# A linear-attention and MLP block on one core: own tile for the last group's sums, a low part behind the first addition, output weights behind the reciprocals, another bank

## The chip, the core and the metric

The kernel runs on one core of a Trainium2 chip. A core has TensorE for matrix products (PE in the profile; its weight loads are PEld), VectorE (DVE), ScalarE (ACT), GpSimd (POOL) and SyncE (SP), which here issues nearly all DMAs. Each engine works off its own queue in order and waits for the others by semaphores. PE writes into PSUM, eight banks of 128 x 512 float32 numbers; DVE and ACT read the banks and free them. The metric is the device time of one execution in microseconds (us); a lower time is better.

## What is computed

One block with two branches on the same normalized input; S = 2048 tokens, D = 640 channels, 32 heads of 20, a hidden layer of 1728, all in float32:

```python
def reference(A_x, A_wqkv, A_w_phi, A_wo, B_x, B_w1, B_b1, B_w2, B_b2):
    x = A_x
    xn = _layernorm(x, axis=-1)
    return x + _A_ref(xn, A_wqkv, A_w_phi, A_wo) + _B_ref(xn, B_w1, B_b1, B_w2, B_b2)

def _A_ref(x, wqkv, w_phi, wo):
    q, k, v = ...                       # x @ wqkv, split into 32 heads
    pq, pk = q @ w_phi, k @ w_phi       # by head
    phi_q = concat(softmax(pq), softmax(-pq))
    phi_k = concat(softmax(pk), softmax(-pk))
    num = phi_q @ (phi_k^T v)
    den = phi_q . sum_s(phi_k) + 1e-6
    return (num / den) @ wo

def _B_ref(x, w1, b1, w2, b2):
    y = _layernorm(x, axis=-1)
    return gelu(y @ w1 + b1) @ w2 + b2
```

## The kernel before

**Split products.** Every float32 operand is split exactly into two parts of the type float32r: a high part, which ACT rounds, and a low part, the rest, which DVE or POOL subtracts (`split`, line 51). A product of two operands takes three matmuls (`mm3`): high by high on line 64, high by low on line 65, low by high on line 66. Nearly all of PE's work has these three lines, in the MLP, the projections and the output product alike.

**The MLP.** Tokens are cut into four blocks `b` of 512, the hidden layer into seven groups `g` of two tiles `j` of 128 (the last group has one and a half). A pass (`passes`, line 255) has two halves: the first layer for the two tiles (five triples of matmuls each into one bank, then gelu on ACT, its high part on ACT and its low part on DVE), and behind a `yield` the second layer: five output tiles `m`, each of six matmuls into a bank, which DVE adds to the accumulator `acc` (line 295 in the first group, 297 later). The halves of neighbouring passes interlock: the first half of a pass is written ahead of the second half of the pass before it. So the low parts of a pass are needed only one pass later. Three banks (0, 1, 2, called `ph`) serve the first layer, two (3, 4, `px`) whatever runs beside it, three (5, 6, 7, `po`) the second layer; output tile `m` + 3 can start only when the addition of tile `m` is done.

**Beside the MLP.** `beside` is a generator, one step of which is taken after each triple; with it, other work is laced into the queues of PE, ACT, DVE and POOL at fixed places, whose order on these engines is the order of writing. What runs beside is, in turn: the transposes of the second token block (`next_y`, line 408, to which `make_y01` belongs, line 173 for the transposes); the preparation of folded weights (L467) and of the later token blocks (`prep`, L563 to L572); then the end of the key-value sums (`finish_kv`, products on lines 866 and 876); and the attention itself (`attend`). The order on SP is a scheduler's.

**Attention.** For each block, `groups` runs through group 10 (the last two heads, and the sums by which the quotients are formed) and then groups 0 to 9: `first` splits the features (L921 on ACT, L922 on POOL), `second` multiplies them with the key-value matrix (L928, L929), copies half of the bank to the tile `ts` on ACT (L938) and adds the other half to it on DVE (L939). For group 10 the result itself stands in `ts`, and two DMAs store it from there (L941, L942). `quotients` then collects the sums through DRAM, takes reciprocals (`dt`, L957), loads them in five transfers into the tile `rx` (L962, L965, L967), spreads them over partitions (L973 on DVE) and multiplies (L975 on POOL).

**Output product.** The weight `wo`, split earlier, is loaded back by `load_wo` (L1004, L1006) into the slots `w3`, `w1`, `r1`, `r2` when the pass (6, 2) has begun; `late` holds a raw copy of `wo` in two pieces (L1040) for sums of weights, with which the output product of blocks 2 and 3 saves matmuls. The output product follows the last pass, in two loops over output tiles.

Of the kernel before, what the change touches and what calls it, by code (L numbers as in the profile page):

```python
# [8 lines left out]
F32 = mybir.dt.float32  # L9
# [31 lines left out]
def f(ap):  # L41
    return ap.bitcast(F32)
# [3 lines left out]
def tile_kernel(ctx: ExitStack, tc: tile.TileContext, x, xT, wkT, wqT, wv, wphi, wo, w1, b1, w2, b2,  # L46
# [152 lines left out]
    class Mlp:  # L199
        def __init__(self, slots, hid):  # L200
            self.hid, self.turn, self.slots, self.beside, self.raw = hid, 0, slots, iter(()), {}
            self.ph, self.px, self.po = Banks(0, 1, 2), Banks(3, 4), Banks(5, 6, 7)

# [47 lines left out]
        def gelu(self, g, j, pz, gt, hh, hl):  # L251
            self.last = nc.scalar.activation(gt, pz, AF.Gelu_apprx_tanh, bias=b1t[:, 2 * g + j:2 * g + j + 1]).ins  # L252
            split(hh, hl, gt)

        def passes(self, g, b, ws, hid=None):
# [27 lines left out]
            for m in range(KC):  # L283
                pw = self.po()
                ms = slice(m * P, (m + 1) * P)
                for j, (hh, hl) in enumerate(hid):
                    w2h, w2l = ws[j][2:]
                    if hl is not None:
                        mm3(pw, w2h[:, ms], w2l[:, ms], hh, hl, j == 0, j == 1)
                        next(self.beside, None)  # L290
                    else:
                        nc.tensor.matmul(pw, w2h[:, ms], hh, start=False, stop=False)
                        nc.tensor.matmul(pw, w2l[:, ms], hh, start=False, stop=True)
                if g == 0:
                    nc.vector.scalar_tensor_tensor(acc[b][:, m, :], pw, b2t[:, m:m + 1], acc[b][:, m, :], op0=ALU.add, op1=ALU.add)
                else:
                    nc.vector.tensor_tensor(acc[b][:, m, :], pw, acc[b][:, m, :], op=ALU.add)  # L297

# [101 lines left out]
    for i in range(4):  # L400
        scale(4 + i, x1[i])
        zs[i]()
    for st in (s23, s47):
        step(st, 1)
# [3 lines left out]
    def next_y():  # L408
        ptile = Banks(3, 4, 0, 1)
        for _ in range(6):  # L410
            yield
        for half in range(2):
            for i, _ in enumerate(make_y01(1, half, x1[2 * half:2 * half + 2], ptile)):
                for _ in range(4 if (half, i) == (0, 1) else 2):
                    yield

    mlp.beside = next_y()
# [425 lines left out]
    def finish_kv(pxt):  # L843
# [30 lines left out]
        tp = pxt()  # L874
# [5 lines left out]
    class Attention:  # L880

        def __init__(self, b, bank):
            self.b, self.n, self.bank = b, 0, bank
            self.ob = op.tile([P, KC, 512], F32, name=f"ob{b}") if b < 2 else acc01.tile([P, KC, 512], F32, name=f"acc{b - 2}")
            self.ts = ep.tile([P, 512], F32, name="ts")
# [39 lines left out]
        def second(self, g, w, ph, pl):  # L925
# [9 lines left out]
            else:  # L935
                a, z = slice(0, 42), slice(64, 106)
                t = o = self.ts[a, :]
# [6 lines left out]
        def quotients(self):  # L944
# [54 lines left out]

    def load_wo():  # L1000

        for p, wd in enumerate(wo_dram):
            w = wp.tile([P, 4, D], F32R, name=f"w{(3, 1)[p]}")
            nc.sync.dma_start(f(w), wd[:, 0:4, :])  # L1004
            last = rp.tile([P, D], F32R, name=f"r{1 + p}")
            nc.sync.dma_start(f(last), wd[:, 4, :])  # L1006
            wol.append([w[:, kc, :] for kc in range(4)] + [last])
# [16 lines left out]
    wol, phs = [], []  # L1024
    ep = op = rx = None

    def attend():
# [73 lines left out]
    for g in range(7):  # L1101
        for b in range(2, 4):
# [17 lines left out]
            if (g, b) == (6, 2):  # L1120
                load_wo()
# [199 lines left out]
```

## Time and profile before

| | us |
|---|---|
| median of three runs | 725.42 |
| lowest and highest run | 723.91, 726.64 |
| the profiled execution | 726.09 |
| its span in the trace | 724.3 |
| PE idle for DVE, POOL (sum of the waits) | 8.9 |
| first matmul after the span's start | 1.3 |

Each row of a timeline has the start and the length in us, the engine, the line, the operation, what it writes and reads, and in brackets how long the engine sat idle before it and for whom. Matmuls overlap: each is shown until its result stands, but the next one starts earlier. In the view of waits a row says which line waited for which, for how long in all, how often, and the longest one. The TensorE clock was granted in full (1.00) throughout.

### The profile page before, as it was taken

Reading aid. Unit: us, or ns where it says so; the run is one execution under the profiler, and the core shown is the slowest. Engines: PE = TensorE matmul, PEld = TensorE weight load, DVE = VectorE, ACT = ScalarE, POOL = GpSimd, SP = SyncE. Lnnn points to the kernel's source line nnn. Section 1 sums busy time; section 2 is a strip of 40 time slices with the busy share of each in tenths; the row PEclk is TensorE's granted clock in tenths of the full one; section 3 lists DMA queues with packets and bytes.
Section 4 is the critical chain, followed back from the end, with each engine's and each line's share of the span. In section 5 each row is a group of like instructions: output and inputs, shape, how many; then the busy total and the mean of one; then the engine's idle time right before and its main releaser. Section 6 shows DMA issues by size and latency. Waiting matters only on the chain.

```text
span 724.3 us, 9717 instructions
## 1 busy us (share of the span) xinstructions
PE 712.1 (98%) x3402; PEld 598.0 (83%) x3402; DVE 488.0 (67%) x824; ACT 333.5 (46%) x569; POOL 388.7 (54%) x342
## 2 busy tenths in 40 slices
PE   9999999999999999999999999999999999999998
PEld 7788888778888888888888888777878778878887
DVE  7846655765554798798788798535574656869753
ACT  6624445433313563464454458346554556551310
POOL 2211222555202896896888878455586677554400
PEclk9999999999999999999999999999999999999999
DMA  9803675455151223723600705863435443163222
GB/s 326 273 19 108 191 198 183 172 179 179 64 209 82 93 71 151 178 91 148 144 1 11 171 1 196 223 159 100 124 109 164 139 145 106 43 233 117 78 82 88
DMA packets 67146, 96.86 MB, mean 134 GB/s; under 512 B 14657, under 2 KB 37841, under 8 KB 65473
## 3 DMA queue, kind: packets, MB, share of 16 engines
q1 hardware_dynamic: 66808, 96.23, 42.7%
q8 instruction: 27, 0.44, 0.3%
q14 instruction: 23, 0.18, 0.1%
q10 hardware_dynamic: 288, 0.01, 0.0%
HBM read 65.87 MB, written 30.35 MB: 133 GB/s over the span
## 4 chain that ended last, share of the span: by engine, by line
PE 77%; DMA 7%; POOL 4%; DVE 4%; issue 3%; ACT 3%; SPq 2%; POOLq 0%; DVEq 0%; ACTq 0%
PE bank L64 23%; PE bank L65 23%; PE bank L66 23%; DMA rx<-d 2%; PE bank L704 2%; DMA r<-in_w 2%; PE bank L467 2%; POOL w L58 1%; PE bank L929 1%; PE bank L928 1%; DMA xb<-in_x 1%; POOL ob L975 1%; DMA e<-e 1%; DVE st L130 1%; DMA o<-ts 1%
## 5 line engine op out<-in xcount | busy, mean ns | idle before, releaser
L58 POOL TENSOR_TENSOR w<-r,w 128x640 fp32r<-128x640 f32 x52 | 84.6, 1645 | 120.2 <-ACT w L55 89.8
L64 PE MATMUL bank<-y,w 128*128 128x512 f32 (+1 forms) x310 | 120.5, 389 | 0.0
L66 PE MATMUL bank<-y,w 128*128 128x512 f32 (+1 forms) x310 | 120.2, 388 | 0.0
L65 PE MATMUL bank<-y,w 128*128 128x512 f32 (+1 forms) x310 | 120.1, 388 | 0.0
L64 PE MATMUL bank<-m,w 128*128 128x512 f32 x266 | 105.6, 397 | 3.8 <-DVE acc L297 3.7
L66 PE MATMUL bank<-m,w 128*128 128x512 f32 x266 | 104.1, 391 | 0.0
L65 PE MATMUL bank<-m,w 128*128 128x512 f32 x262 | 102.4, 391 | 0.0
L58 DVE TENSOR_TENSOR m<-m,m 128x512 fp32r<-128x512 f32 (+1 forms) x54 | 45.0, 833 | 72.3 <-ACT m L55 72.2
L297 DVE TENSOR_TENSOR acc<-bank,acc 128x512 f32<-128x512 f32 x120 | 80.5, 682 | 16.4 <-PE bank L66 11.6
L64 PE MATMUL bank<-wkh,y 128*128 128x512 f32 (+2 forms) x240 | 87.6, 365 | 0.0
L65 PE MATMUL bank<-wkl,y 128*128 128x512 f32 (+2 forms) x240 | 87.1, 363 | 0.0
L66 PE MATMUL bank<-wkh,y 128*128 128x512 f32 (+2 forms) x240 | 86.9, 362 | 0.0
L65 PEld LDWEIGHTS bank<-y,w 128*128 128x128 f32 x310 | 58.3, 188 | 12.1
L66 PEld LDWEIGHTS bank<-y,w 128*128 128x128 f32 x310 | 58.2, 188 | 12.1
L64 PEld LDWEIGHTS bank<-y,w 128*128 128x128 f32 x310 | 58.2, 188 | 12.0
L669 POOL TENSOR_TENSOR m<-m,mx 128x640 f32<-128x640 f32 (+2 forms) x48 | 44.5, 940 | 42.7 <-DVE mx L657 42.7
L650 ACT ACTIVATE m<-bank 128x512 f32<-128x512 f32 (+1 forms) x64 | 26.5, 440 | 85.5 <-PE bank L66 59.6
L64 PEld LDWEIGHTS bank<-m,w 128*128 128x128 f32 x266 | 50.0, 188 | 17.1 <-DVE acc L297 6.9
L252 ACT ACTIVATE m<-bank,b1t 128x512 f32<-128x512 f32 (+1 forms) x54 | 36.3, 672 | 53.3 <-PE bank L66 50.7
L922 POOL TENSOR_TENSOR e<-e,m 120x512 fp32r<-120x512 f32 (+1 forms) x28 | 38.1, 1361 | 39.6 <-ACT m L921 39.0
L66 PEld LDWEIGHTS bank<-m,w 128*128 128x128 f32 x266 | 49.9, 188 | 10.7
L676 DVE TENSOR_REDUCE sm<-m 128x64 f32<-128x1280 f32 x32 | 47.3, 1479 | 15.9 <-ACT m L674 15.7
(213 smaller groups left out, 1468.2 us busy)
## 6 DMA issues: line engine op xcount, KB each, us to landing
r<-in_w SPq DMA_DIRECT2D x52, 320.0 KB
e<-e SPq DMA_DIRECT2D x40, 240.0 KB
e<-acc SPq DMA_DIRECT2D x52, 160.0 KB
acc<-in_xT SPq DMA_DIRECT2D x4, 1280.0 KB
xb<-in_x SPq DMA_DIRECT2D x8, 320.0 KB
t<-in_x SPq DMA_DIRECT2D x8, 320.0 KB
raw<-in_xT SPq DMA_DIRECT2D x10, 256.0 KB
yh<-t SPq DMA_DIRECT2D x10, 256.0 KB
```

Source lines behind the costliest of these rows:

```text
L58: eng.tensor_tensor(lo, src, f(hi), op=ALU.subtract)
L64: nc.tensor.matmul(ps, lh, rh, start=first, stop=False, **kw)
L65: nc.tensor.matmul(ps, lh, rl, start=False, stop=False, **kw)
L66: nc.tensor.matmul(ps, ll, rh, start=False, stop=last, **kw)
L252: self.last = nc.scalar.activation(gt, pz, AF.Gelu_apprx_tanh, bias=b1t[:, 2 * g + j:2 * g + j + 1]).ins
L297: nc.vector.tensor_tensor(acc[b][:, m, :], pw, acc[b][:, m, :], op=ALU.add)
L467: nc.tensor.matmul(ps[:, c + i * kd:c + (i + 1) * kd], raw[n, g][:kk, (kc + i) * P:(kc + i + 1) * P], wpt[:kk, g, :kd // DF, 1:], start=Tr ...
L650: return nc.scalar.activation(p3[:, :, c], ps.rearrange("p (h f) -> p h f", h=H), AF.Copy).ins
L669: subs[n, t] = nc.gpsimd.tensor_tensor(ep[:, s], a, b, op=ALU.subtract)
L676: nc.vector.tensor_reduce(sm, e.rearrange("p s (h f) -> p (s h) f", f=DH), axis=AX, op=ALU.add)
L704: nc.tensor.matmul(kvp[g // 2][:VM, (g % 2) * 240:(g % 2) * 240 + 240].rearrange("p (s f) -> p s f", s=4), v[:, g * VS:g * VS + VM], ft[:, ...
L922: nc.gpsimd.tensor_tensor(pl, e, f(ph), op=ALU.subtract)
```

## The change

Five edits.

1. Group 10's sums get a tile of their own, `rest`, in place of `ts`.
2. With the flag `hold`, the gelu of the second tile of a pass makes its high part at once, but its low part is kept back until the first addition of the second layer that is written next. The flag is set for the passes from (1, 0) on, left out for (2, 0), and in the second part of the kernel, which handles blocks 2 and 3, set from the attention on, at (1, 2): 20 low parts move.
3. At the start, the transposes `next_y` begin three steps later, and the last of four scalings of x goes from DVE to ACT, behind the gelus.
4. The third product of `finish_kv` (L876) takes its bank from `ph` (it becomes bank 0) where it took one from `px` (bank 3, which the first product had).
5. Of `load_wo` the two large loads move into `quotients` of the last block, behind the last load of reciprocals; the two small ones stay where they were (`load_last`). The two raw pieces of `wo` are issued later, at steps 24 and 28 of block 2's groups in place of 8 and 16.

```diff
         def gelu(self, g, j, pz, gt, hh, hl):
             self.last = nc.scalar.activation(gt, pz, AF.Gelu_apprx_tanh, bias=b1t[:, 2 * g + j:2 * g + j + 1]).ins
-            split(hh, hl, gt)
+            if self.hold and j == 1:
+                nc.scalar.activation(hh, gt, AF.Copy)
+                self.held.append(lambda: nc.vector.tensor_tensor(hl, gt, f(hh), op=ALU.subtract))
+            else:
+                split(hh, hl, gt)
...
                     nc.vector.tensor_tensor(acc[b][:, m, :], pw, acc[b][:, m, :], op=ALU.add)
+                while self.held:
+                    self.held.pop()()
...
     for i in range(4):
-        scale(4 + i, x1[i])
+        if i < 3:
+            scale(4 + i, x1[i])
         zs[i]()
+    scale(7, x1[3], True)
...
         ptile = Banks(3, 4, 0, 1)
-        for _ in range(6):
-            yield
-        for half in range(2):
-            for i, _ in enumerate(make_y01(1, half, x1[2 * half:2 * half + 2], ptile)):
-                for _ in range(4 if (half, i) == (0, 1) else 2):
+        for _ in range(9):
+            yield
+        for half, waits in enumerate(((3, 1, 1), (2, 2, 2))):
+            for n, _ in zip(waits, make_y01(1, half, x1[2 * half:2 * half + 2], ptile)):
+                for _ in range(n):
                     yield
 
-    mlp.beside = next_y()
+    mlp.beside, mlp.hold = next_y(), True
...
             this = mlp.passes(g, b, ws)
+            mlp.hold = (g, b) != (2, 0)
             next(this)
...
-        tp = pxt()
+        tp = mlp.ph()
...
-            self.ts = ep.tile([P, 512], F32, name="ts")
+            self.ts, self.rest = ep.tile([P, 512], F32, name="ts"), ep.tile([42, 512], F32, name="rest")
...
-                t = o = self.ts[a, :]
+                t = o = self.rest
...
-                nc.sync.dma_start(rx[o + 2::64], rden[30:32].unsqueeze(1).to_broadcast([2, KC, 512]))
+                last = nc.sync.dma_start(rx[o + 2::64], rden[30:32].unsqueeze(1).to_broadcast([2, KC, 512])).ins
                 yield
+            if self.b == NB - 1:
+                with tc.issue_after(last):
+                    load_wo()
...
-                    if b == 2 and i in (8, 16):
-                        j = i // 16
+                    if b == 2 and i in (24, 28):
+                        j = i // 28
...
-                mlp.beside = attend()
+                mlp.beside, mlp.hold = attend(), True
...
             if (g, b) == (6, 2):
-                load_wo()
+                load_last()
```

On PE, in the program's first part (`xb` are the token tiles, `y` the normalized input, `w_171` the second hidden tile's weights, `m` the hidden layer), there stands before, at the first transposes:

```order
L64 MATMUL bank_425<-y_141,w_171 128x512
L65 MATMUL bank_425<-y_142,w_171 128x512
L66 MATMUL bank_425<-y_141,w_171 128x512
L173 MATMUL bank_432<-idt,xb 128x128 x4
L64 MATMUL bank_425<-y_141,w_171 128x512
```

and now, three triples further on:

```order
L64 MATMUL bank_425<-y_141,w_171 128x512
L65 MATMUL bank_425<-y_142,w_171 128x512
L66 MATMUL bank_425<-y_141,w_171 128x512
L173 MATMUL bank_441<-idt,xb 128x128 x4
L64 MATMUL bank_450<-m_146,w_168 128x512
```

The first transposes have moved from inside the second tile's first layer to its end, right ahead of the second layer.

On DVE, at the end of the preparation (`raw` are columns of x, `m_1528` is the low part of the second gelu, `acc` the accumulator), before:

```order
L58 TENSOR_TENSOR m_1501<-m_1500,m_1501 128x512
L563 TENSOR_TENSOR raw<-raw,m_1247 128x512
L58 TENSOR_TENSOR m_1528<-m_1500,m_1528 128x512
L570 TENSOR_TENSOR raw<-raw,t 128x512
L297 TENSOR_TENSOR acc_99<-bank_1550,acc_99 128x512
L297 TENSOR_TENSOR acc_99<-bank_1564,acc_99 128x512
```

and now (line numbers of the changed kernel: 572 and 579 are the former 563 and 570, 302 is the former 297, 256 is the low part kept back):

```order
L58 TENSOR_TENSOR m_1501<-m_1500,m_1501 128x512
L572 TENSOR_TENSOR raw<-raw,m_1247 128x512
L579 TENSOR_TENSOR raw<-raw,t 128x512
L302 TENSOR_TENSOR acc_99<-bank_1549,acc_99 128x512
L256 TENSOR_TENSOR m_1528<-m_1500,m_1528 128x512
L302 TENSOR_TENSOR acc_99<-bank_1564,acc_99 128x512
```

The low part has moved behind the first addition; the other rows keep their order.

On SP, ahead of the output product (`dt` and `rx` are the reciprocals, `woh` and `wol` the split output weights), before:

```order
L958 DMA d_95<-dt 128x128
L962 DMA rx<-d_95 4x2560
L1004 DMA w_5849<-woh 128x2560
L1004 DMA w_5853<-wol 128x2560
L965 DMA rx<-d_95 2x2560
L967 DMA rx<-d_95 2x5x512
L965 DMA rx<-d_95 2x2560
L967 DMA rx<-d_95 2x5x512
```

and now:

```order
L968 DMA d_95<-dt 128x128
L972 DMA rx<-d_95 4x2560
L975 DMA rx<-d_95 2x2560
L977 DMA rx<-d_95 2x5x512
L975 DMA rx<-d_95 2x2560
L977 DMA rx<-d_95 2x5x512
L1024 DMA w_5891<-woh 128x2560
L1024 DMA w_5893<-wol 128x2560
```

The two loads of the weights have moved behind all five transfers of the reciprocals. At block 1's reciprocals the two pieces of `wo` (L1040 before), of which one stood between the transfers, both stand behind them now.

More of the change, by code (lines that the diff above doesn't have):

```diff
@@ L202, in __init__ @@
             self.ph, self.px, self.po = Banks(0, 1, 2), Banks(3, 4), Banks(5, 6, 7)
+            self.hold, self.held = False, []
         def fetch(self, c, pool=None):
@@ L998, in split, with load_last @@
                 nc.sync.dma_start(acc[b], a_dram[b])
+    def load_last():
+        for p, wd in enumerate(wo_dram):
+            last = rp.tile([P, D], F32R, name=f"r{1 + p}")
+            nc.sync.dma_start(f(last), wd[:, 4, :])
+            lasts.append(last)
     def load_wo():
@@ L1004, in load_wo @@
             nc.sync.dma_start(f(w), wd[:, 0:4, :])
-            last = rp.tile([P, D], F32R, name=f"r{1 + p}")
-            nc.sync.dma_start(f(last), wd[:, 4, :])
-            wol.append([w[:, kc, :] for kc in range(4)] + [last])
+            wol.append([w[:, kc, :] for kc in range(4)] + [lasts[p]])
     def first_split():
@@ L1022, in both @@
             yield
-    wol, phs = [], []
+    wol, lasts, phs = [], [], []
     ep = op = rx = None
```

## The prediction

> **What bounds the kernel now.** I read the page's first part, then the waits of TensorE (PE), then the timeline of PE around each wait.
>
> ```profile
> PE 712.1 (98%) x3402; PEld 598.0 (83%) x3402; DVE 488.0 (67%) x824; ACT 333.5 (46%) x569; POOL 388.7 (54%) x342
> PE bank L64 <- DVE acc L297: 3.7, 5, 1.4
> PE bank L173 <- DVE xb L164: 1.7, 2, 1.4
> PE bank L876 <- DVE km L858: 1.4, 1, 1.4
> PE bank L929 <- POOL e L922: 0.8, 1, 0.8
> ```
>
> PE works 98% of the span and no other engine comes near it. The matmuls are not changed, so only PE's holes can be won. The view of waits gives four kinds: the second-layer matmuls (L64) wait for a PSUM bank that an addition (L297) has not yet emptied, transposes (L173) wait for a scaled x, L876 waits for its bank, and one attention matmul (L929) waits for its low part. Together 7.6 us, but a hole costs more than its idle time, as one of them shows.
>
> ```profile
> 488.35 0.40 PE L66 MATMUL bank<-m,w 128*128 128x512 f32 x1
> 490.20 0.50 PE L64 MATMUL bank<-m,w 128*128 128x512 f32 x1 [1.45 <-DVE acc L297]
> 490.53 0.40 PE L65 MATMUL bank<-m,w 128*128 128x512 f32 x1
> 490.76 0.39 PE L66 MATMUL bank<-m,w 128*128 128x512 f32 x1
> ```
>
> In full flow a 512-column matmul starts 0.23 us after the one before (490.53 to 490.76), though each is shown 0.40 long. Before the hole the step is 490.20 - 488.35 = 1.85, so 1.62 is lost, and the next step (0.33) loses 0.10 more: 1.72 for 1.45 of idle. So I add 0.27 to each idle time, or 0.16 where the next step is a normal one.
>
> ```profile
> 26.38 0.55 PE L173 MATMUL bank<-idt,xb 128*128 128x128 f32 x3 [1.42 <-DVE xb L164]
> 131.39 0.50 PE L64 MATMUL bank<-m,w 128*128 128x512 f32 x1 [0.33 <-DVE acc L297]
> 159.17 0.50 PE L64 MATMUL bank<-m,w 128*128 128x512 f32 x1 [0.28 <-DVE acc L297]
> 460.83 0.56 PE L876 MATMUL bank<-sel,kxs 107*80 107x30 f32 x6 [1.37 <-DVE km L858]
> 539.90 0.40 PE L66 MATMUL bank<-m,w 128*128 128x512 f32 x1
> 540.36 0.50 PE L64 MATMUL bank<-m,w 128*128 128x512 f32 x1
> 573.17 0.51 PE L64 MATMUL bank<-m,w 128*128 128x512 f32 x1 [0.78 <-DVE acc L297]
> 586.68 0.50 PE L929 MATMUL bank<-e,kvs 120*128 120x512 f32 x1 [0.78 <-POOL e L922]
> 650.80 0.50 PE L64 MATMUL bank<-m,w 128*128 128x512 f32 x1 [0.88 <-DVE acc L297]
> ```
>
> The prices: 1.58 at 26 us, 0.60 at 131, 0.55 at 159, 1.53 at 461, 1.72 at 490, 0.33 at 540 (a step of 0.46 for 0.23, and 0.10), 1.05 at 573, 1.05 at 587, 1.15 at 651. **Ceiling: 9.6 us.** Each hole is now asked whether the change closes it, and what comes next there.
>
> **The transposes (26 us), -1.4.** The first ones move from behind the 7th first-layer triple to behind the 10th, three triples of 3 x 0.23 later.
>
> ```profile
> 24.69 0.27 PE L173 MATMUL bank<-idt,xb 128*128 128x128 f32 x1
> 25.79 0.54 DVE L164 TENSOR_SCALAR xb<-xb,ry 128x640 f32<-128x640 f32 x1
> 27.05 0.42 DVE L58 TENSOR_TENSOR m<-m,m 128x256 fp32r<-128x256 f32 x1
> 28.36 0.69 ACT L252 ACTIVATE m<-bank,b1t 128x512 f32<-128x512 f32 x1 [1.49 <-DVE ra L153]
> ```
>
> They would start at 24.69 + 2.04 = 26.73; the second x they need is scaled at 26.33. The hole goes. But PE now reaches the second layer at about 27.1 (26.73 and some 0.4 for four transposes, an estimate from the 0.55 that three take with their modelled tail), and its second matmul, 0.23 later, needs the low part that DVE ends at 27.47: I charge 0.2 for that; bounds 0 and 0.5. The last scaling, moved from DVE to ACT, falls into the 1.49 that ACT waits for DVE ahead of the next gelu, and shortens that wait by the 0.54 that DVE no longer spends on it. I count nothing for it; without that cover ACT would be late by a scaling, somewhat over the 0.69 of a gelu.
>
> **Low part behind the addition (131, 159), -1.15.** In the 20 places where the order of DVE changes, the low part of the second gelu stands behind the first addition.
>
> ```profile
> 157.22 0.69 DVE L58 TENSOR_TENSOR m<-m,m 128x512 fp32r<-128x512 f32 x1 [1.94 <-ACT m L55]
> 158.44 1.28 DVE L297 TENSOR_TENSOR acc<-bank,acc 128x512 f32<-128x512 f32 x2
> ```
>
> DVE sat idle for 1.94 with the addition queued behind a low part that waited for ACT. Without it the addition can run up to 1.94 sooner, and sooner by the 0.69 of the low part in any case; 0.55 was missing. At 131 the order changes in the same way, and 0.60 was missing, less than a low part. Both holes go; bounds 0 and 1.15. The low part itself is read only in the next block's second layer, many us later.
>
> **Bank of L876 (461), -1.4.** Three products share two banks, so the third waited for DVE to read the first. Taken from the three banks of the first layer, it starts at once. Next in line is the first attention group:
>
> ```profile
> 473.73 1.29 POOL L922 TENSOR_TENSOR e<-e,m 80x512 fp32r<-80x512 f32 x1 [12.70 <-ACT m L921]
> 476.56 0.40 PE L929 MATMUL bank<-e,kvs 80*128 80x512 f32 x1
> ```
>
> POOL ends at 475.02, on a chain from loads that do not move with PE. PE asked at 476.56 and will ask at 476.56 - 1.53 = 475.03: just met, so I charge 0.1; bounds 0 and 1.5.
>
> **Own tile for the sums (490), -1.7.** The sums of group 10 stood in the tile `ts`, which the next group overwrites.
>
> ```profile
> 479.53 4.57 DMA o<-ts
> 484.21 0.60 ACT L938 ACTIVATE ts<-bank 64x512 f32<-64x512 f32 x1 [6.10 <-PE bank L66]
> ```
>
> The chain of waits shows ACT held until the store had read `ts` (the bracket names the wrong one of several waits); a gelu, a low part and the addition came late behind it. With `rest` ACT can go on up to 6.1 us sooner, as soon as PE has filled the bank; 1.72 was missing. Bounds 0 and 1.72.
>
> **The output weights' pieces (573), -1.05, and what hangs on it (587), -0.3.**
>
> ```profile
> 563.22 0.39 SPq L1040 DMA_DIRECT2D woc<-in_wo  x1
> 564.86 6.64 DMA rx<-d
> 571.63 0.01 DVE L973 LOAD_MASK_SELECT rx<-rx  x1 [1.82 <-DMA rx<-d]
> 572.47 2.67 POOL L975 TENSOR_TENSOR ob<-ob,rx 128x512 f32<-128x512 f32 x2 [1.36 <-DVE rx L973]
> 584.90 1.73 POOL L922 TENSOR_TENSOR e<-e,ph 120x512 fp32r<-120x512 f32 x1
> ```
>
> A 655 KB piece of `wo` was issued between the reciprocals' transfers, the last of which took 6.64; DVE waited 1.82 for it with an addition behind. Both pieces now go behind. If the last transfer lands over 1.5 us sooner, the hole at 573 closes (-1.05). POOL then starts up to 1.36 sooner on a chain that ran full until it ended at 586.63. PE's demand also comes 1.05 sooner, so only 1.36 - 1.05 = 0.3 is won at 587; bounds 0 and 1.05.
>
> At 540 DVE has the same work ahead of the second addition in either order: 0.1, bounds 0 and 0.33.
>
> **Weights behind reciprocals (651), -1.15.**
>
> ```profile
> 638.59 0.39 SPq L1004 DMA_DIRECT2D w<-woh  x1
> 641.13 8.16 DMA rx<-d
> 649.42 0.01 DVE L973 LOAD_MASK_SELECT rx<-rx  x1 [1.52 <-DMA rx<-d]
> 655.46 0.39 PE L64 MATMUL bank<-y,w 128*128 128x512 f32 x1
> ```
>
> Two loads of 1.3 MB stood ahead of four of the five reciprocal transfers, and DVE waited 1.52 with an addition behind it. Now they stand behind. From the first load's issue to the last transfer's lie 2.54 us and five issues, 0.51 each, so the loads go out some 2.1 later. The last transfer, behind them, landed at 649.29; if the loads had landed by then, they now do by 651.4. PE will want them at 655.46 - 1.15 = 654.3: covered by 2.9, and beyond that each late us costs one. The trace bounds their landing from above only by PE's use at 655.46 without a wait; at that end the cost is 655.46 + 2.1 - 654.3 = 3.3. I take the nearer row, no cost.
> [...]
>
> **Sum.** 1.4 + 1.15 + 1.4 + 1.7 + 1.05 + 0.3 + 0.1 + 1.15 = 8.25; I keep back 0.25 for small new holes at the 20 moved low parts. 726.09 (the profiled execution's own time; its span is 724.3) - 8.0 = 718.1. The median before is 725.42, 0.67 lower, and gives 717.4 by the same gain. I state 717.8.
>
> **Rivals.**
> (1) *Part of the holes re-forms one step later*, because the chains of DMA, POOL and DVE behind them have their own clock. For it: the 475.02 against 475.03 above, the 27.47, POOL's full chain at 587. Against it: where DVE or ACT waited, they had idle time. If 461 and 587 give nothing, half of 26 and 573 is lost, and 0.5 is lost elsewhere, the gain is 8.25 - 1.4 - 0.3 - 0.7 - 0.5 - 0.5 = 4.85: 721.
>
> (2) *The change does not reach the waits*: the reciprocals' transfers may be slow by themselves, and ACT may be late for other reasons. Then 490, 573, 587 and 651 stay, and 8.0 - 1.7 - 1.05 - 0.3 - 1.15 = 3.8 is won: 722. Against it: 6.64 and 8.16 have large loads just ahead.
>
> (3) *Slower: the moved low parts lock POOL and DVE against each other.*
>
> ```profile
> 535.23 1.60 DVE L58 TENSOR_TENSOR m<-m,m 128x512 fp32r<-128x512 f32 x1
> L58 DVE TENSOR_TENSOR m<-m,m 128x512 fp32r<-128x512 f32 x50 | 42.3, 846 | 72.1 <-ACT m L55 71.9
> ```
>
> A low part with POOL at work took 1.60 against a mean of 0.85, 0.75 more. Standing between the first two additions it could push the second one past the point at which PE needs its bank. Twenty times 0.75 is 15; above 8.25 / 20 = 0.41 each the kernel gets slower, and with all of it the time is 726.1 - 8.25 + 15 = 733. Against it: with three banks PE needs the second tile's bank four tiles of 6 x 0.23 after the layer's first matmul, at 5.5 us; that tile is complete at 2.8, and 2.7 us hold a stretched low part (1.60) and an addition (half of the 1.28 above).
> [...]
>
> **Chances.** Forecast 0.68, (1) 0.20, (2) 0.09, (3) 0.03. The range: low end, all 9.6 from the median and 0.2 of scatter, 715.6; high end, rival (1) at 721 and 0.6 of scatter, 721.6; the 3.3 of late weights lies within it. Half a per cent is 3.6 us, about what a measurement of this kernel can tell from no change. The forecast and most of (1) lie beyond it: faster 0.86, same 0.11, slower 0.03.
>
> **What would show it.** The waits of PE should hold no row of L876 and at most small ones for L297 and L929; the row ACT from DMA `o<-ts` should be gone; the last `rx` transfer should take 2 to 5 us instead of 6.64 and 8.16; POOL should still release L929 near 580 with some tenths. PE's first matmul with the output weights should come without a gap. Wrong would be: a wait of PE for DMA there, low parts near 1.6 followed by waits for L297, or holes closed with the span unchanged, which would mean that PE's steps grew.

## The result and the profile after

The changed kernel takes **717.69 us** in the median of its runs (717.33 to 718.51) against 725.42 before (723.91 to 726.64): a ratio of 0.9894 with a 95% interval of 0.9878 to 0.991. That is 1.1% faster. The forecast was 717.8. The profiled execution took 717.33 us with a span of 715.5, against 726.09 and 724.3.

The page's first part and the view of TensorE's waits, of the changed kernel (us in total, times, longest):

```profile
PE 709.7 (99%) x3402; PEld 597.9 (84%) x3402; DVE 494.2 (69%) x823; ACT 334.1 (47%) x570; POOL 388.2 (54%) x342
PE bank L373 <- POOL m L371: 1.3, 1, 1.3
PE bank L173 <- DVE xb L164: 0.8, 2, 0.4
PE bank L939 <- POOL e L932: 0.3, 1, 0.3
PE bank L64 <- DVE acc L302: 0.2, 1, 0.2
```

L64's waits for an addition went from 3.7 to 0.2, those for the scaled x from 1.7 to 0.8, the one for the bank of L876 (now L886) is gone, and the attention's (L939, once L929) is 0.3 in place of 0.8. The first row (L373) is the start, and was there before. Gone from the views of the other engines' waits are these two rows of the kernel before:

```profile
ACT ts L938 <- DMA o<-ts: 3.1, 1, 3.1
DVE rx L973 <- DMA rx<-d: 3.3, 2, 1.8
```

Both kernels issue the same 3402 matmuls, in the same order but for the first transposes. So the start of one and the same matmul in the two traces tells how far ahead the changed kernel is there, its lead in us. The lead just ahead of each hole and just behind it gives what the hole brought; between the holes it drifts by 0.2 in all.

| hole (time before) | lead ahead of it, behind it | won | forecast |
|---|---|---|---|
| transposes, 26 | 0.03, 1.47 | 1.4 | 1.4 |
| addition, 131 | 1.45, 1.59 | 0.1 | 0.60 |
| addition, 159 | 1.57, 2.12 | 0.55 | 0.55 |
| bank of L876, 461 | 2.16, 3.73 | 1.57 | 1.4 |
| sums of group 10, 490 | 3.76, 5.48 | 1.7 | 1.7 |
| addition, 540 | 5.51, 5.85 | 0.34 | 0.1 |
| reciprocals, 573 | 5.83, 6.88 | 1.05 | 1.05 |
| GpSimd's low part, 587 | 6.89, 7.39 | 0.50 | 0.3 |
| addition, 621 | 7.45, 7.57 | 0.12 | none |
| reciprocals, 651 | 7.61, 8.76 | 1.15 | 1.15 |

At the end the lead is 8.79, the difference of the two spans. Two holes are left. The one at 131 came back 1.5 us further on, 0.43 in size, so that only 0.1 is won there. VectorE (DVE) there, from its timeline:

```profile
127.58 1.15 DVE L58 TENSOR_TENSOR wkl<-raw,wkh 128x640 fp32r<-128x640 f32 x1 [1.84 <-ACT wkh L55]
128.66 0.68 DVE L302 TENSOR_TENSOR acc<-bank,acc 128x512 f32<-128x512 f32 x1
129.26 1.27 DVE L256 TENSOR_TENSOR m<-m,m 128x512 fp32r<-128x512 f32 x1
130.45 0.68 DVE L302 TENSOR_TENSOR acc<-bank,acc 128x512 f32<-128x512 f32 x1
```

and TensorE's two waits of that kind, from its timeline:

```profile
131.19 0.50 PE L64 MATMUL bank<-m,w 128*128 128x512 f32 x1 [0.15 <-DVE acc L302]
579.29 0.50 PE L939 MATMUL bank<-e,kvs 120*128 120x512 f32 x1 [0.28 <-POOL e L932]
```

The first addition (128.66) now runs ahead of the low part, but a `wkl` that waited 1.84 for ScalarE still stands ahead of it, and the low part moved behind it (L256) takes 1.27. So the **second** addition ends at 131.13, and TensorE waits for that one. At 579 GpSimd's chain of multiplications and low parts still ends a little late.

At the output weights the forecast feared a late landing. TensorE and the DMA engines there, in windows (us, busy time of each engine, granted clock, DMA share, GB/s):

```profile
640.00:645.00 5.00, 5.00 (x24) 4.14 (x23) 4.65 (x11) 1.06 (x3) 2.69 (x4) 1.00 0.95 389
645.00:646.00 1.00, 1.00 (x7) 0.81 (x6) 0.64 (x2) 0.00 (x0) 1.00 (x1) 1.00 0.15 61
646.00:648.00 2.00, 2.00 (x10) 1.69 (x9) 2.00 (x6) 0.00 (x0) 1.03 (x2) 1.00 0.00 0
```

and the first matmul that reads them:

```profile
646.68 0.39 PE L64 MATMUL bank<-y,w 128*128 128x512 f32 x1
```

The transfers stop soon after 645, and TensorE asks at 646.68: some 1.5 us of cover, and no wait. How long the last transfer of reciprocals now takes can't be read, since nobody waits for it; VectorE's use of it bounds it only at 6.8 us there (7.4 in block 2).

### The profile page after: what moved, and what is told of

The parts are those of the page before. It is cut to its first block, busy times and chain, and to the rows that moved or that the text cites. A ratio compares the mean times of both kernels' runs of the same rounds, so it can differ in the third digit from the quotient of the medians.

```text
span 715.5 us, 9759 instructions
## 1 busy us (share of the span) xinstructions
PE 709.7 (99%) x3402; PEld 597.9 (84%) x3402; DVE 494.2 (69%) x823; ACT 334.1 (47%) x570; POOL 388.2 (54%) x342
## 4 chain that ended last, share of the span: by engine, by line
PE 95%; DVE 2%; POOL 1%; DMA 1%; issue 0%; ACT 0%
PE bank L64 28%; PE bank L65 28%; PE bank L66 28%; PE bank L714 3%; PE bank L476 2%; PE bank L939 1%; PE bank L938 1%; PE bank L298 1%; PE bank L279 1%; PE bank L278 1%; PE bank L297 1%; PE bank L343 1%; PE bank L173 1%; DMA e<-e 0%; DVE st L130 0%; DMA xb<-in_x 0%
## 5 line engine op out<-in xcount | busy, mean ns | idle before, releaser
L64 PE MATMUL bank<-y,w 128*128 128x512 f32 (+1 forms) x310 | 120.4, 388 | 0.0
L64 PE MATMUL bank<-m,w 128*128 128x512 f32 x266 | 105.1, 395 | 0.2 <-DVE acc L302 0.2
L64 PE MATMUL bank<-wkh,y 128*128 128x512 f32 (+2 forms) x240 | 87.7, 365 | 0.0
L64 PEld LDWEIGHTS bank<-y,w 128*128 128x128 f32 x310 | 58.3, 188 | 12.0
L64 PEld LDWEIGHTS bank<-m,w 128*128 128x128 f32 x266 | 50.0, 188 | 11.2 <-DVE acc L302 0.8
L58 DVE TENSOR_TENSOR m<-m,m 128x512 fp32r<-128x512 f32 (+1 forms) x34 | 27.9, 823 | 44.1 <-ACT m L55 43.9
```

The source lines that it names most:

```text
L58: eng.tensor_tensor(lo, src, f(hi), op=ALU.subtract)
L64: nc.tensor.matmul(ps, lh, rh, start=first, stop=False, **kw)
```

## The experiments

Twelve kernels, each one or two edits away from the changed kernel or from the one before. The kernel before ran beside all of them, in three sets, 63 times, with a median of 724.81. Its median is 723.73 in the first set, 724.54 in the second and 725.48 in the third; the changed kernel ran in none of them. So a difference of a us or less between a row and the changed kernel's is no difference that the times show, and the sizes below come from the traces. All times:

| kernel | runs | median us | lowest, highest | runs with a granted clock under 0.999 |
|---|---|---|---|---|
| before | 63 | 724.81 | 721.99, 728.54 | 37 |
| changed | 5 | 717.69 | 717.33, 718.51 | 0 |
| sums in `ts` | 4 | 717.99 | 717.86, 719.11 | 0 |
| low parts ahead | 4 | 718.30 | 717.87, 719.29 | 0 |
| both of these | 7 | 719.91 | 718.76, 721.10 | 0 |
| pieces early | 4 | 717.68 | 717.40, 719.03 | 0 |
| pieces early, low parts ahead | 7 | 719.31 | 717.74, 720.29 | 0 |
| weights early | 7 | 721.07 | 717.79, 723.17 | 3 |
| weights early, twice | 9 | 722.05 | 718.54, 723.63 | 7 |
| before, weights behind | 12 | 724.10 | 721.35, 728.13 | 6 |
| before, two early edits | 10 | 724.49 | 721.25, 728.61 | 4 |
| two early edits undone | 12 | 724.57 | 720.56, 726.04 | 10 |
| low parts twice | 10 | 722.55 | 722.37, 723.75 | 0 |
| low part behind the second addition, spaced | 5 | 717.00 | 716.23, 718.19 | 0 |

### The hole at 490: own tile, or the moved low part?

Three kernels: the sums back in `ts`,

```diff
-                t = o = self.rest
+                t = o = self.ts[a, :]
```

> The changed kernel, with the sums of group 10 back in the tile ts; all else stays. Theory A (each edit closes a hole of its own, gains add): the hole that stood at 490 us returns whole, at about 485 us, 1.7 us; span about 717.2. Theory B (two edits share this hole): the store of ts ends at about 480.8 (the sums end at 475.0 now, and from there to the end of the store the trace of before shows 5.8), the second sum of group 1 then ends at about 484.7 and the first addition, which no longer stands behind a low part, at 485.4; TensorE asks for its bank at 484.8, so the hole is 0.6 of idle and some 0.25, 0.85 us; span about 716.4. Theory C (the addition's move alone closes it): no hole, span 715.5.

the low parts ahead of the additions,

```diff
-            if self.hold and j == 1:
+            if False and j == 1:
```

> The changed kernel, with every low part of a second gelu ahead of the first addition again; own tile and the rest stay. Theory A: the holes at 159 (0.55), 540 (0.3) and 621 (0.17) return, at 131 the old one (0.60) takes the place of the new one (0.43); about 1.2 us in all, span about 716.7; none at 485, since ACT is not held there. Rival (with the other waits gone the low parts in front cost nothing): within 0.3 of 715.5. Second rival (the low part in front also makes a hole at 485): more than 2 us, span over 717.5.

and both.

> The changed kernel with both undone: the sums in ts and the low parts ahead. Theory A (gains add): 1.7 and 1.2, span about 718.4, that is, the losses of the two single runs added. Theory B (two edits share the hole at 485): the same 718.4, but more than the two single losses added, by about 0.85, and the hole at 485 is 1.7 here and about 0.85 with the sums in ts alone. Theory C: hole at 485 only here.

With the sums in `ts`, ScalarE's timeline shows the old wait for the store:

```profile
480.00 0.59 ACT L948 ACTIVATE ts<-bank 64x512 f32<-64x512 f32 x1 [5.18 <-DMA d<-ts]
```

But the addition, free of the low part, follows soon, and VectorE's timeline of the same kernel has it ahead of it:

```profile
483.14 0.69 DVE L949 TENSOR_TENSOR ob<-bank,ts 64x512 f32<-64x512 f32 x1 [0.45 <-ACT ts L948]
483.86 0.69 DVE L302 TENSOR_TENSOR acc<-bank,acc 128x512 f32<-128x512 f32 x1
484.52 0.69 DVE L256 TENSOR_TENSOR m<-m,m 128x512 fp32r<-128x512 f32 x1
```

Between 484 and 487 TensorE loses 0.7 in two small steps (0.2 and 0.5), not 1.7. With the low parts ahead and the own tile kept it loses nothing there. With both undone it loses 2.6: 0.5 at 483 and 2.1 at 487.8, in TensorE's timeline of that kernel

```profile
487.76 0.50 PE L64 MATMUL bank<-m,w 128*128 128x512 f32 x1 [1.85 <-DVE acc L302]
```

So **theory B** holds: two edits close one hole, each covers most of it without the other, and the losses do not add. By spans, one execution of each kernel: 0.4 and 1.1 alone, 3.1 together.

The low parts ahead alone bring the holes back at 159 (0.55), 536 (0.34) and 614 (0.11), nothing on balance at 131, as theory A of that run said. This execution has one hole more, 0.52 at 474, where ScalarE waited 4.5 for the first attention group's load, against 3.3 in the changed kernel, and 0.4 less at 579, where TensorE comes later. The kernel with both edits undone does not have the hole at 474, so I count it as chance.

### The pieces of `wo`

```diff
-                    if b == 2 and i in (24, 28):
-                        j = i // 28
+                    if b == 2 and i in (8, 16):
+                        j = i // 16
```

> The changed kernel with the two pieces of wo issued at steps 8 and 16 of the third block's groups again, between the transfers of the reciprocals. Theory A (the piece in front of the transfers delays them): the last rx transfer takes about 6.6 us again, the hole of 1.05 returns at about 566 and the one at 579 grows from 0.53 to about 1.05; 1.6 us in all, span about 717.1. Rival 1 (the low part's move or the earlier TensorE had opened these places): the holes stay closed, 715.5. Rival 2 (the hole at 566 returns but POOL's chain is set by its own work): 1.1 us or less with the one at 579 at 0.5 or smaller, since TensorE asks later.

Theory A **fell**, and the first rival stands: 717.68 and a span of 715.1, no hole at 566, and the one at 579 no larger. VectorE's timeline of this kernel shows why it need not wait:

```profile
561.06 0.69 DVE L302 TENSOR_TENSOR acc<-bank,acc 128x512 f32<-128x512 f32 x1 [0.78 <-PE bank L66]
561.67 1.80 DVE L256 TENSOR_TENSOR m<-m,m 128x512 fp32r<-128x512 f32 x1
563.50 0.70 DVE L949 TENSOR_TENSOR acc<-bank,ts 64x512 f32<-64x512 f32 x1
564.12 0.01 DVE L986 LOAD_MASK_SELECT rx<-rx  x1
```

The moved low part (1.80 here) now stands ahead of the reciprocals, so VectorE comes to them later, and the transfer is there. To see whether that alone covered it, the low parts went ahead again as well.

> The changed kernel with the pieces of wo early and the low parts ahead, so that VectorE comes to the reciprocals as early as before. Theory A (the early piece does delay the transfer, and in the run with the pieces alone the moved low part covered it: VectorE came to the transfer 1.1 us later): VectorE waits for the last rx transfer by 1 us or more, a hole of 0.7 to 1.1 returns at about 567, on top of the 0.7 to 1.1 that the low parts ahead cost alone; span 717.2 to 717.7. Theory B (the 6.64 of the profile of before was chance, one slow packet): no wait for it over 0.3, no hole at 567; span 716.2 to 716.6.

Still no hole at 567, and VectorE does not wait for the transfer:

```profile
566.05 0.01 DVE L986 LOAD_MASK_SELECT rx<-rx  x1
```

(Its 1.9 us over the changed kernel's span come from 131, where low parts of 1.57 and 1.91 in front of the addition made a hole of 1.6 in that execution, and from 159 and 536 as before.) Two later kernels, made from the one before, keep piece and low part early too; their holes were 0.60 and 0.53. With the 1.05 of the first profile and the 0 here that makes four traces of one place, from 0 to 1.05. **The size of this hole differs from trace to trace, and its mean, 0.55, is half of what I charged.** These are four kernels with one execution each, so that chance makes the difference is likely, but not separated from the other edits. That the piece takes part is possible, since it stood early in all four; no run shows it.

### The output weights

```diff
-            if self.b == NB - 1:
-                with tc.issue_after(last):
-                    load_wo()
...
-                load_last()
+                load_last()
+                load_wo()
```

> The changed kernel with both loads of the output weights ahead of the reciprocals' transfers again. Theory A (the loads delay the transfers): the last rx transfer takes about 8 us again, VectorE waits 1.5 for it, and the hole at about 642 returns, 1.2 us; span about 716.7. Rival (as with the pieces of wo, the transfer's time in the profile of before was not due to the load ahead of it, or VectorE now comes to it later for other reasons): no hole at 642, span 715.5 and the two loads' packets end before the transfers' anyway.

Median 721.07, and the runs lie 5.4 us apart, where the changed kernel's lie 1.2 apart. The profiled execution is the fastest of the seven; its VectorE waits little:

```profile
640.92 0.01 DVE L983 LOAD_MASK_SELECT rx<-rx  x1 [0.66 <-DMA rx<-d]
```

The last transfer, issued at 632.78, is there at 640.9: 8.1 us, as the 8.16 before, against at most 6.8 in the changed kernel. So theory A is right about the transfer. What differs between the traces is the chain of small transfers ahead of it (store the sums, load them, store the reciprocals, load them), and with 8 us behind it no time is left to take that up. The hole is 0.3 in this profile, 1.15 in that of before and 2.8 in another one below, where the transfer itself also took longer, 8.9. In the median this edit undone costs 3.4; its four runs at full clock alone reach from 717.79 to 721.07. The opposite, this edit alone on the kernel before:

> The kernel before with the output weights behind the reciprocals alone. Theory S (spread): the chain of small transfers that ends at the last rx transfer takes a few us more or less from one execution to the next; with the 8 us of the weights in its way this reaches TensorE at about 650, at 1.15 in the profile of before but at about 3 on average; so the median falls by about 3, to 721.5 against 724.5, and the runs lie closer together than the 6.3 of before (722.2 to 728.5), with no granted clock under 0.999. Theory P (the price of the profile): the median falls by 1.2, to 723.3, and the spread stays. The profile is also a second look at the other holes of before: 1.58 at 26, 1.53 at 461 and 1.72 at 490 should be there within 0.3; the one of 1.05 at 573, if it was chance, should be gone or under half.

The median of this kernel is 724.10, against 725.48 of the kernel before run beside it: 1.4, near the 1.2 of theory P, but with an interval of the ratio of 0.9963 to 1.0, which reaches to no gain. In the trace the hole at 651 is gone, 1.15 us. **Theory S fell**: the runs still spread from 721.35 to 728.13, and half have a lowered clock. Its profile shows one place where that comes from. TensorE's timeline behind the hole of L876:

```profile
458.81 0.40 PE L66 MATMUL bank<-m,w 128*128 128x512 f32 x1
460.89 0.56 PE L876 MATMUL bank<-sel,kxs 107*80 107x30 f32 x6 [1.69 <-DVE km L858]
...
462.32 0.39 PE L65 MATMUL bank<-y,w 128*128 128x512 f32 x1
462.55 0.49 PE L66 MATMUL bank<-y,w 128*128 128x512 f32 x1
462.84 0.63 PE L64 MATMUL bank<-y,w 128*128 128x512 f32 x1
463.27 0.63 PE L65 MATMUL bank<-y,w 128*128 128x512 f32 x1
```

and its windows around it (the granted clock is the third number from the right):

```profile
457.00:461.00 4.00, 2.31 (x16) 1.72 (x15) 3.13 (x5) 1.02 (x3) 3.64 (x2) 1.00 0.96 226
461.00:463.00 2.00, 2.00 (x13) 1.68 (x14) 1.93 (x7) 0.80 (x3) 0.09 (x1) 0.93 0.96 232
463.00:467.00 4.00, 4.00 (x13) 3.16 (x12) 0.88 (x3) 0.05 (x1) 0.00 (x0) 0.61 0.97 231
467.00:473.00 6.00, 6.00 (x28) 4.96 (x27) 1.58 (x3) 2.64 (x4) 0.00 (x0) 1.00 0.98 244
```

The first matmuls behind the hole still start 0.23 apart. From 462.7 on, 1.8 us behind it, a matmul starts 0.43 after the last, for some 3.4 us: **TensorE idled, and soon after its granted clock fell**, to 0.61 in the mean of 463 to 467. It costs 1.6 here, of which a part comes back: the hole of 1.72 at 490, which was expected to be found again within 0.3, is not there. VectorE's addition ends at 489.07, 1.1 earlier than in the profile of before, and TensorE needs it only at 490.26:

```profile
488.38 0.69 DVE L297 TENSOR_TENSOR acc<-bank,acc 128x512 f32<-128x512 f32 x1
490.26 0.39 PE L64 MATMUL bank<-m,w 128*128 128x512 f32 x1
```

Without the 1.6 TensorE would have asked at some 488.6, and waited. The other holes of before are there as expected (1.58 at 26, 1.8 at 461), and the one at 573 is 0.53, half its size. To see the clock at the other place, a kernel whose hole at 642 should be long:

```diff
+            for _ in range(2):
+                nc.sync.dma_start(f(w), wd[:, 0:4, :])
-            nc.sync.dma_start(f(w), wd[:, 0:4, :])
```

(with the loads early, and each issued twice).

> The changed kernel with the output weights ahead of the transfers, and each of the two loads issued twice, so that the hole at 642 becomes long in every execution: 2.6 MB more at some 0.42 MB per us are 6.2 us, so a hole of 6.5 to 9.5. Theory C (a long hole also lowers TensorE's granted clock behind it): granted clock 0.995 to 0.998, the steps behind the hole are longer than 0.23 for some us, and the time is 2 to 4 us above the hole's own length: 726 to 731. Rival (the clock under 0.999 in the longest runs of before has another cause): clock 1.0, steps of 0.23 right behind the hole, 724 to 727.

The repeats did not stand where I wanted them: each waits for the first load of its tile, so they went out behind the transfers. VectorE's wait still grew to 3.6 and TensorE's hole to 2.9:

```profile
643.27 0.01 DVE L983 LOAD_MASK_SELECT rx<-rx  x1 [3.62 <-DMA rx<-d]
```

The windows of this kernel:

```profile
641.00:645.00 4.00, 1.27 (x6) 0.77 (x5) 1.72 (x4) 0.00 (x0) 0.85 (x1) 0.87 0.94 361
645.00:651.00 6.00, 6.00 (x15) 4.63 (x15) 3.43 (x8) 0.00 (x0) 2.98 (x3) 0.52 0.79 319
651.00:657.00 6.00, 6.00 (x28) 4.91 (x27) 5.76 (x10) 0.00 (x0) 4.24 (x4) 1.00 0.02 6
```

15 matmuls fall into 6 us at a granted clock of 0.52, where 28 do at 1.00. With a lower clock of one half, as the steps of 0.43 for 0.23 have it, the windows' 0.87 and 0.52 make 6.8 us of it, from 644.0, still in the hole, to 650.8, at a cost of 3.0 on top of the hole's 2.9. Theory C holds for the clock (0.995 in this execution, 0.998 in six others, 1.0 in two) and for the steps. The hole is under half of what I expected, and so the median, 722.05, lies below the range.

Idle times of 1.69 and 2.73 us stand ahead of these two stretches of long steps. A hole of a length between them stands without one:

```profile
648.17 0.50 PE L64 MATMUL bank<-m,w 128*128 128x512 f32 x1 [2.57 <-DVE acc L297]
648.51 0.39 PE L65 MATMUL bank<-m,w 128*128 128x512 f32 x1
648.74 0.40 PE L66 MATMUL bank<-m,w 128*128 128x512 f32 x1
```

This is TensorE's timeline of the kernel before with the two early edits: 2.57 idle, and full speed right behind, with steps of 0.23 from the second one on and a granted clock of 1.00 from 648 to 654. The clock also differs between executions of one kernel: with the weights early three of seven runs have 0.997 or 0.998, the others 0.999 or 1.0. What decides it, no run here shows.

### The two early edits (transposes, bank)

Alone on the kernel before, and undone in the changed kernel (the edits are those of the change, at `next_y`, `scale(7, ...)` and `tp = mlp.ph()`; for the bank, undone):

```diff
-        tp = mlp.ph()
+        tp = pxt()
```

> The kernel before with the later transposes and the other bank alone. Gains add: the holes at 26 and 461 close, 1.5 + 1.55 = 3.05 us, span about 721.3 against 724.3; all the later holes (131, 159, 490, 540, 573, 587, 651) are found again about 1.5 to 3 earlier with the sizes of before. Rival (gains are taken back by the chains behind): under 2.3 us, with a larger wait at the first attention group (about 473) or at 487. On the transfers: theory A says the last rx transfers take 6.6 and 8.2 us again and the holes of 1.05 and 1.15 stand; theory B (chance) says at least one of them is gone or under half its size.

> The changed kernel with the early transposes and the bank from the two again. Theory A (what the traces showed at the two holes, 1.5 and 1.55, reaches the end): median 720.7, span 718.6. Theory B (part of it is given back behind, where transfers set the pace, as the two edits alone brought nothing that the times could tell): the two holes are there in the trace, but the end moves by 1.5 or less, median 719.2 or lower; then later holes of the changed kernel (579, 131) are smaller here.

In the traces both holes behave as forecast: alone, TensorE is 3.4 ahead behind 461 (0.2 of it from the start); undone, 3.7 behind (the hole at 461 is 2.5 in that execution, with 2.26 of idle time, and the steps behind it stay at 0.23):

```profile
460.79 0.56 PE L884 MATMUL bank<-sel,kxs 107*80 107x30 f32 x6 [2.26 <-DVE km L866]
```

In the times neither theory of either run fits. **Alone, the pair brings nothing that can be told** (0.9996, 0.9967 to 1.0025); **undone, it costs 6.9** (724.57 against 717.69), with 10 of 12 runs at a lowered clock. Its two runs at full clock took 720.56 and 721.21, 2.9 and 3.5 over the changed kernel: there the 3.05 of the two holes is found. The clock is a part of the rest: its eight runs at 0.997 to 0.998 have a median of 724.58, 3.7 above these two, and 0.002 of 723 us is some 1.4. The other 2 us are not explained; longer holes in those executions would do it, but the only trace kept of this kernel is at full clock. As the two edits were always made or undone together, the hole at 26 is not separated from the one at 461. The pair alone leaves the hole at 651, which in its profile is 2.8 long, since VectorE waits 3.47 for the transfer behind the weights:

```profile
646.81 0.01 DVE L975 LOAD_MASK_SELECT rx<-rx  x1 [3.47 <-DMA rx<-d]
```

On the transfers neither theory of the run with the pair alone holds: the hole at 573 is 0.60, a little over half, and the one at 651 grew. Why the pair's six runs at full clock (median 723.57) are hardly below those of the kernel before run beside it (15, median 723.84) is only half explained by that one profile, and stays open.

### How much room the moved low part has

```diff
-                self.held.append(lambda: nc.vector.tensor_tensor(hl, gt, f(hh), op=ALU.subtract))
+                self.held += 2 * [lambda: nc.vector.tensor_tensor(hl, gt, f(hh), op=ALU.subtract)]
```

> The changed kernel in which every low part that stands behind the first addition is computed twice on VectorE, one after the other: twenty extra operations of 0.69 us or more between the first and the second addition. Main theory (2.7 us of room between the first addition and the second one's due time, counted in three banks): only the places where a low part is stretched already (131, 484, 564) lose some; 1 to 3 us, span 716.5 to 718.5. Rival (what stands there counts in full, or VectorE and GpSimd lock each other at each place): 0.41 us or more at each of the twenty, over 8 us, span over 723.5.

The span grows by 4.9 us, between the theories. Groups of VectorE in this kernel, and the timeline at the place where the pair is longest:

```profile
L256 DVE TENSOR_TENSOR m<-m,m 128x512 fp32r<-128x512 f32 x40 | 38.6, 966 | 0.7
```

```profile
516.03 3.57 DVE L256 TENSOR_TENSOR m<-m,m 128x512 fp32r<-128x512 f32 x2
519.52 0.67 DVE L949 TENSOR_TENSOR ob<-bank,ts 64x512 f32<-64x512 f32 x1
520.12 1.27 DVE L302 TENSOR_TENSOR acc<-bank,acc 128x512 f32<-128x512 f32 x2
```

Twenty more operations of 0.97 are 19.3 us of VectorE; a quarter of it reaches TensorE, in seven holes of 0.5 to 1.1. At 516 the two take 1.8 each. In the changed kernel's trace the 20 single ones fall into three kinds: eight with GpSimd idle beside them took 0.67 to 0.68; beside the other twelve GpSimd was at work for 0.68 or more, and of these six took 0.68 to 0.71 and six 1.27 to 1.81. So GpSimd was at work beside every long one, but beside short ones too; what stretches a low part is not shown. Once, a stretched low part fits ahead of the second addition; twice, not. So the room between first and second addition is real, but only 13 of the 20 places hold a second low part; 7 do not.

### Two more moves

```diff
-                while self.held:
+                while self.held and m > 0:
...
-                for i in range(2):
+                for i in range(2 if self.b == NB - 1 else 3):
                     yield
```

> The changed kernel with two more moves: the low part of the second gelu behind the second addition instead of the first, and the multiplications of the quotients in the first three blocks three steps apart instead of two, so that GpSimd has room for the attention groups' low parts between them. Theory: the hole at 131 (0.1 to 0.43) and the one at 579 (0.53) close and nothing comes in their place; span 714.8, median 716.9. Rival (as at 131, a hole re-forms one step on: a third addition behind the low part, or VectorE's shuffles next to the later additions): span 715.3 or more, median 717.5 or more.

Median 717.00, span 715.1. No wait for an addition or a low part is left in the view of TensorE's waits:

```profile
PE bank L373 <- POOL m L371: 1.3, 1, 1.3
PE bank L173 <- DVE xb L164: 0.8, 2, 0.5
```

VectorE's timeline at the first of the two places:

```profile
128.71 1.27 DVE L302 TENSOR_TENSOR acc<-bank,acc 128x512 f32<-128x512 f32 x2
129.91 0.68 DVE L256 TENSOR_TENSOR m<-m,m 128x512 fp32r<-128x512 f32 x1
```

Two additions run back to back and the low part follows, 0.68 long where it was 1.27. Both holes are gone, and a small one of 0.2 stands at 472, at the first attention group. Over all 20 places the moved low parts take 1.28 in the mean, against 0.99 in the changed kernel, but TensorE waits for none of them. By the times it can't be told from the changed kernel (its runs overlap); against the kernel before it is 0.9882 (0.9863 to 0.9901).

## Why the prediction was right, step by step

The holes' sum, 8.25, was right against the 8.8 that the two traces differ by, and the method with it: PE's start-to-start excess is what a hole costs. That the sum comes so close is luck in part: 131 gave 0.1 of its 0.60, others gave 0.1 to 0.2 more than charged, and the 1.55 won at 573 and 587 did not come from the edit that it was charged to. Point by point:

- **Transposes, bank (1.4 each).** Right in the trace: 1.4 and 1.57. The feared new wait at the second layer is there and small (27.5 us, 0.3). The next attention group was met without a wait.
- **Low part behind the addition (1.15 for 131 and 159).** 159 gave 0.55. **The 0.60 at 131 is the step that failed**: "Both holes go" looked at the first addition alone. The low part moved behind it is ahead of the second one, and a `wkl` kept its place in front of both; the hole came back one output tile later, 0.43 in size. It is the first rival, at one place. The low part behind the second addition closes it.
- **Own tile (1.7).** Right size, wrong ownership: beside the moved low parts the tile is worth 0.4 to 0.7, because they close most of the same hole; without them it is worth 2.1 (the spans 718.7 and 716.6). I had priced each edit as if the others were not there.
- **Pieces of `wo` (1.05) and GpSimd's chain behind (0.3).** The holes closed by 1.05 and 0.50, but not because of this edit: undone, it costs nothing, with the moved low parts or without. In the run without them VectorE uses the last transfer 5.25 us after its issue and does not wait, so it took less than the 6.64 of before with the piece just as early. What closed the hole is not isolated; with the moved low parts VectorE also comes later.
- **Weights behind reciprocals (1.15).** Right in the trace, 1.15, and right that PE gets its weights in time (a cover of 1.5, where I had 2.9). Undone, it costs 3.4 in the median: with the weights early the hole was 0.3, 1.15 and 2.8 in three traces, and three of the seven runs have a lowered clock.
- **The slower rival.** The moved low parts (L256, groups of the changed kernel by shape) are longer than those left in place, 0.99 against 0.84, and still cost nothing but the 131 hole. Doubled, they cost 0.24 each, below the 0.41 at which that rival would have decided.

```profile
L58 DVE TENSOR_TENSOR m<-m,m 128x512 fp32r<-128x512 f32 x30 | 25.3, 844 | 43.8 <-ACT m L55 43.6
L256 DVE TENSOR_TENSOR m<-m,m 128x512 fp32r<-128x512 f32 x20 | 19.9, 993 | 0.0
```

**Two things were left out of the sum, with opposite signs.** The profiled execution of before, 726.09, was at full clock, and still 2.3 above 723.79, the median of the 26 later runs at full clock. So its holes were probably larger than the usual ones; that is argued, since only one trace of this kernel is kept, and the full-clock medians of the three later sets differ too (722.96, 723.84, 724.82). And 37 of 63 runs have a lowered clock; with them the median is 724.81. The profile showed none of it. So against the later 724.81 the gain is 7.1, and against the 725.42 measured beside the changed kernel 7.7, where the sum gave 8.0.

## What to carry to other kernels

Price a hole from the start-to-start steps, then ask for each edit which other edit closes the same hole, and what then stands ahead of the next tile. A hole that hung on a chain of small transfers had no fixed size here (0.3, 1.15 and 2.8 at one place, 0 to 1.05 at another): look at several executions, and at the spread of the times, before charging it. And the last one or two long holes were worth more than their length here, with TensorE busy for 98 to 99% of the span: the two early edits undone cost 6.9 where the trace shows 3.7, and the clock stayed at 0.999 or more in all 46 runs without the holes at 461 and 651, where 67 of the 113 with one or both were below.

## What the runs showed of the hardware

The granted clock fell at holes with 1.69 and 2.73 us of idle time (to 0.61 and 0.52 in the windows behind them, with steps of 0.43 for 0.23, for some 3.4 and 6.8 us, at a cost of 1.6 and 3.0). Behind others with 2.26 and 2.57 the steps stayed at 0.23; in the window behind the 2.57 the granted clock is 1.00. In the runs of the kernel before, the times go with it: a median of 723.79 at a clock of 0.999 or 1.0 (26 runs), 725.41 at 0.997 to 0.998 (27), 727.7 at 0.995 (10). It is not the clock alone, since of these 27 the ten at 0.997 have the lower median, 724.30 against 725.94. None of the 46 runs of the eight kernels whose holes at 461 and 651 were both closed was under 0.999, even with a hole of 2.1 at 488. What decides it at a hole of a given length stays open.

The record of the granted clock does not show everything. In both kernels' traces the first matmuls also start 0.43 apart (up to 7.0 us before, up to 5.3 in the changed kernel), where the record has 1.00; so the clock of the kernel before was full throughout by the record, not by the steps. The changed kernel gains nothing by it: its lead is 0.03 at 24 us.

The chain of small transfers also took up to 1.3 us more in one trace than in another: from the load of the sums' issue to the store of the reciprocals' issue, with VectorE's reciprocal in between, it was 3.5 us before, 4.1 in the changed kernel, 3.3 with the weights early and 4.6 with the two early edits alone.
